# Value stores moved to other queues, two weight loads moved behind the third normalization, and the first tiles normalized in pairs with their root on ScalarE

## The chip, the cores and the metric

The kernel runs on one core of a Trainium2 chip. The metric is the device time of one execution in microseconds (us), and less is better.

The engines are named as in the profile: PE is TensorE (matmuls), PEld its weight loads, DVE is VectorE, ACT is ScalarE, POOL is GpSimd ("Pool" in the text), SP is SyncE, whose queue is called the sync queue here. "ACTq" or "SPq" in a line of the profile is that engine's instruction queue.

## The reference, cut to what matters

The input `x` is 2048 rows of 640. It is normalized once, and two branches read the result: a sliding, dilated attention (32 heads of 20, a window of 8 rows at distance 2) and a gated product of three matrices (F = 1536). Their outputs and `x` are summed.

```python
x  = A_x                                    # (1, 2048, 640) bf16
xn = _layernorm(x)                          # (x - mean) / sqrt(var + 1e-5)
# A: q, k, v = xn @ wqkv; logits over 8 earlier rows (0, 2, ..., 14 back); softmax; weighted v; @ wo
# B: (xn @ w_gate) * (xn @ w_up), then @ w_down
return x + A(xn, wqkv, wo) + B(xn, w_gate, w_up, w_down)
```

## The kernel before: the parts that matter

The 2048 rows are four chunks of four tiles of 128 rows. All engines are scheduled by hand: the program keeps a list for TensorE (`main`), one for VectorE (`chain`) and a list of things that happen when a condition holds (`later`), and a small clock model decides the order in which instructions are emitted. What is emitted on one engine stays in order.

The steps of a chunk that this story needs are:

1. VectorE takes statistics of `x`, Pool takes the root, VectorE scales. The first chunk is transposed on TensorE. Chunks 2 to 4 are stored (`xnD`) and transposed by a DMA (`xnT`).
2. TensorE makes q, k and v. The values go to DRAM (`vD`) and come back, eight shifted rows for each row, as `v8` (two buffers).
3. VectorE multiplies q with eight shifted k (`pw`, eight products a chunk); TensorE adds up the heads (`lps`, called head products here); ScalarE takes the exponential `e`. `e` is stored (`eD`) and comes back transposed by a DMA as `eT`.
4. VectorE normalizes `eT`, then for each tile mixes `v8` with `eT` and adds up. The result is stored and comes back transposed (`oT`) for the output product (`psf`, with `wo_perm`, then `wd`).

```python
    def load_down():
        wo_r = A_wo.rearrange("(h t jl) d -> jl h t d", h=H, t=KT, jl=JL)
        for jl in range(JL):
            nc.gpsimd.dma_start(out=wo_perm[jl * H : (jl + 1) * H, :, :], in_=wo_r[jl])   # 0.8 MB in all
        nc.gpsimd.dma_start(out=wd[:], in_=B_w_down.rearrange("(f p) d -> p f d", p=P))   # 1.9 MB
    # ... cut
            def stats():
                # ... cut: bn_stats, bn_aggr of each tile of the group
                rstd = cpool.tile([P, group], F32, name="rstd", bufs=2)
                nc.gpsimd.tensor_scalar(rstd[:], g["mv"][:, :, 1], EPS, None, op0=ALU.add)
                nc.gpsimd.tensor_tensor(
                    rstd[:], rstd[:], mhalf[:].to_broadcast([P, group]), ALU.pow
                )
                g["rstd"] = rstd
    # ... cut
        if group == 1:               # first chunk: stats 0, stats 1, scale 0, stats 2, scale 1, ...
            prev = None
            for t0 in range(CH):
                cur = steps(t0)
                if prev:
                    prev[0]()
                prev = cur
            prev[0]()
    # ... cut: value product, after the second half of a tile
                    if k == 1:
                        nc.scalar.dma_start(
                            out=vD[HALO + tg * P : HALO + (tg + 1) * P, :], in_=v_t[:]
                        )
    # ... cut
        def keep_e():
            rows = eD[c * 2 * P : (c + 1) * 2 * P, :]
            nc.sync.dma_start(out=rows.rearrange("(g p) t -> p g t", p=P), in_=st["e"][:])
            later.append((turn_e, lambda t=min(clock["pe"], clock["dve"]): t + 3.0))

        def turn_e():
            st["eT"] = apool.tile([P, CH, 2 * P], BF, name="eT")
            rows = eD[c * 2 * P : (c + 1) * 2 * P, :]
            nc.sync.dma_start_transpose(out=st["eT"][:], in_=rows.rearrange("r (t p) -> r t p", p=P))
            done["eT", c] = min(clock["pe"], clock["dve"]) + 7.0
    # ... cut: VectorE's order
    norm(0, 1)
    side(load_ffn)
    norm(1, 4)
    side(constants)
    later.append((lambda: (load_x(2), load_down()), when(("turned", 1))))
    weights(0)
    side(lambda: (want_v8(0), want_v8(1)))
    turned_weights(0)
    norm(2, 4)
    attend(0, range(CH))
    side(lambda: load_x(3))
    weights(1)
    # ... cut: further chunks; TensorE's order:
    vproj(0, range(CH)); qk(0); glu(0); qk(1); vproj(1, range(CH)); qk(2); vproj(2, range(CH)); finish(0)
    # ... cut
```

On VectorE the second chunk's `pw` (`weights(1)`) stands behind all four tiles of the first chunk's attention (`attend(0, ...)`). On TensorE the head products of the second chunk come in as soon as `pw` allows, during or just before `finish(0)`.

The softmax here doesn't subtract the row's maximum and nothing guards it: scores larger than these inputs give would overflow.

## Time and profile before

| | before |
|---|---|
| median of the six runs known at the prediction | 275.74 us (275.15 to 277.23) |
| the run that was profiled | 272.23 us, span 270.5 us |
| PE busy | 261.1 us, 97% |
| query product starts | 17.39 us |
| `eT` lands | 57.06 us (issue 53.56 + 3.5) |
| second chunk's `pw` starts | 87.56 us |

The profiled run is 3.5 us faster than the median.

The page of before. In the rows of slices the span is cut in 40, about 6.8 us each; each digit is a busy share in tenths, PEclk the clock that was granted to TensorE. The last two lines are the chain of work that ended last, by engine and by line.

```profile
span 270.5 us, 4126 instructions
PE 261.1 (97%) x1607; PEld 145.0 (54%) x1624; DVE 202.1 (75%) x258; ACT 101.7 (38%) x181; POOL 34.6 (13%) x72
PEclk9899999999999999999999999999999999999999
DMA  6999999990898975454820896986188498310111
PE 81%; DVE 11%; DMA 5%; SPq 1%; issue 1%; ACT 0%; ACTq 0%
PE psu L556 19%; PE psg L556 19%; PE psf L605 19%; PE psqk L351 8%; PE psf L598 8%; PE psv L377 4%; PE lps L433 4%; DMA v_925<-vD 3%; DVE pw L422 2%; DMA x_t<-in_A_x_dram 2%; DVE v_925 L500 1%; DVE v_607 L500 1%; DVE v_609 L500 1%; DVE v_60
```

PE is busy nearly all the time and carries the chain for 81%. DMA is saturated in the slices from about 7 to 61 us, and idle in the next one.

The head in the timeline of before (start, duration, engine, line, operation, tile; in brackets the idle time before it and what ended it):

```profile
8.26 0.89 DVE L239 BATCH_NORM_STATS2 stats<-x_t 128x6 f32<-128x320 bf16 x2 [2.55 <-DMA x_t<-in_A_x_dram]
9.30 0.39 DVE L261 TENSOR_SCALAR xn_t<-x_t,mv,rstd 128x640 bf16<-128x640 bf16 x1
9.76 0.45 PE L272 MATMUL pst<-ident,xn_t 128*128 128x128 bf16 x5 [1.63 <-DVE xn_t L261]
...
17.39 10.96 PE L351 MATMUL psqk<-xnT,wqkv 128*128 128x512 bf16 x49
```

VectorE works in order. Tile 1's scaling (9.30) was ready by about 6.4 us (its root ends there), but stands behind the statistics of tile 2, whose `x` lands at 8.26. PE waits 1.63 us for it.

The weight loads and the way of the exponentials, in the timeline of before:

```profile
24.62 2.33 POOL L157 DMA_DIRECT2D wo_perm<-in_A_wo_dram  x4
26.94 1.07 POOL L158 DMA_DIRECT2D wd<-in_B_w_down_dram  x1
...
48.91 0.38 SPq L462 DMA_DIRECT2D eD<-e  x1
53.56 1.45 SPq L468 DMA_TRANSPOSE eT<-eD  x1
57.89 1.87 DVE L485 TENSOR_REDUCE rs<-eT 128x128 f32<-128x1024 bf16 x1
```

The weights are issued at 24.6 to 28 us. The exponentials go out at 48.91 and come back transposed at 57.06, and at 57.89 VectorE sums them (`rs`) for its normalization.

The waits of before between 80 and 105 us (who waited for whom: total, times, longest):

```profile
ACT v_t L383 <- DMA oT<-oD: 3.5, 1, 3.5
PE psv L377 <- ACT v_t L383: 1.1, 1, 1.1
PE lps L433 <- DVE pw L422: 0.7, 1, 0.7
```

PE idles 1.8 us here: 1.1 for a PSUM copy that ScalarE does late, and 0.7 for VectorE's `pw`. ScalarE is late because it stands 3.5 us in front of a value store in its queue, and the profile puts this to the landing of an `oT` transpose.

### The profile page before, as it was taken

Reading aid. Unit: us, or ns where it says so; the run is one execution under the profiler, and the core shown is the slowest. Engines: PE = TensorE matmul, PEld = TensorE weight load, DVE = VectorE, ACT = ScalarE, POOL = GpSimd, SP = SyncE. Lnnn points to the kernel's source line nnn. Section 1 sums busy time; section 2 is a strip of 40 time slices with the busy share of each in tenths; the row PEclk is TensorE's granted clock in tenths of the full one; section 3 lists DMA queues with packets and bytes.
Section 4 is the critical chain, followed back from the end, with each engine's and each line's share of the span. In section 5 each row is a group of like instructions: output and inputs, shape, how many; then the busy total and the mean of one; then the engine's idle time right before and its main releaser. Section 6 shows DMA issues by size and latency. Waiting matters only on the chain.

```text
span 270.5 us, 4126 instructions
## 1 busy us (share of the span) xinstructions
PE 261.1 (97%) x1607; PEld 145.0 (54%) x1624; DVE 202.1 (75%) x258; ACT 101.7 (38%) x181; POOL 34.6 (13%) x72
## 2 busy tenths in 40 slices
PE   7799999999999799999999999999999999999995
PEld 7454444444646467644444677744446774445773
DVE  3452796659879996599999979999899979921221
ACT  2455555555653310155555520045551005555000
POOL 3548100400000004300000003020000302000100
PEclk9899999999999999999999999999999999999999
DMA  6999999990898975454820896986188498310111
GB/s 181 332 376 395 257 283 256 377 196 4 224 332 250 270 211 139 157 151 155 262 70 2 262 324 137 266 300 54 39 227 243 128 294 239 125 48 2 48 48 48
DMA packets 54706, 52.18 MB, mean 193 GB/s; under 512 B 24754, under 2 KB 52352, under 8 KB 54688
## 3 DMA queue, kind: packets, MB, share of 16 engines
q1 hardware_dynamic: 49344, 37.82, 51.3%
q0 software_dynamic: 3040, 11.49, 13.3%
q10 hardware_dynamic: 2304, 2.62, 2.7%
q8 instruction: 12, 0.20, 0.3%
q14 instruction: 6, 0.05, 0.1%
HBM read 35.39 MB, written 10.90 MB: 171 GB/s over the span
## 4 chain that ended last, share of the span: by engine, by line
PE 81%; DVE 11%; DMA 5%; SPq 1%; issue 1%; ACT 0%; ACTq 0%
PE psu L556 19%; PE psg L556 19%; PE psf L605 19%; PE psqk L351 8%; PE psf L598 8%; PE psv L377 4%; PE lps L433 4%; DMA v_925<-vD 3%; DVE pw L422 2%; DMA x_t<-in_A_x_dram 2%; DVE v_925 L500 1%; DVE v_607 L500 1%; DVE v_609 L500 1%; DVE v_607 L516 1%; DVE v_925 L516 1%
## 5 line engine op out<-in xcount | busy, mean ns | idle before, releaser
L556 PE MATMUL psu<-xnT,wu 128*128 128x512 bf16 x240 | 59.7, 379 | 0.0
L556 PE MATMUL psg<-xnT,wg 128*128 128x512 bf16 x228 | 59.0, 379 | 0.6
L605 PE MATMUL psf<-wd,hT 128*128 128x320 bf16 x384 | 57.4, 299 | 0.0
L561 ACT CAST gs<-psg 128x512 bf16<-128x512 f32 x48 | 28.1, 585 | 70.7 <-PE psg L556 69.7
L422 DVE TENSOR_TENSOR pw<-qT,kT 128x2560 bf16<-128x2560 bf16 x32 | 46.3, 1485 | 6.8 <-ACT kT L357 6.8
L605 PEld LDWEIGHTS <-hT 128*128 128x128 bf16 x384 | 37.5, 98 | 14.7 <-DVE hT L566 0.2
L351 PE MATMUL psqk<-xnT,wqkv 128*128 128x512 bf16 x195 | 43.9, 379 | 0.3
L556 PEld LDWEIGHTS <-wu 128*128 128x128 bf16 x240 | 23.3, 98 | 28.7 <-issue 0.8
L556 PEld LDWEIGHTS <-wg 128*128 128x128 bf16 x240 | 23.3, 98 | 28.2 <-issue 0.8
L561 ACT CAST us<-psu 128x512 bf16<-128x512 f32 x48 | 28.1, 585 | 25.9 <-PE psu L556 25.9
L566 DVE TENSOR_TENSOR hT<-gs,us 128x512 bf16<-128x512 bf16 x48 | 19.8, 418 | 16.6 <-ACT us L561 16.2
L351 PEld LDWEIGHTS <-wqkv 128*128 128x128 bf16 x200 | 19.4, 98 | 23.6 <-issue 0.8
L622 POOL DMA_DIRECT2D out_dram<-osb x13 | 7.2, 557 | 185.0 <-DVE osb L612 185.0
L612 DVE TENSOR_TENSOR osb<-psf,xr 128x320 bf16<-128x320 f32 x32 | 15.3, 486 | 20.5 <-PE psf L605 17.2
L598 PE MATMUL psf<-wo_perm,oT 128*128 128x320 bf16 x160 | 27.0, 299 | 0.0
L377 PE MATMUL psv<-wqkv,xnT 128*128 128x320 bf16 x160 | 24.4, 308 | 1.2 <-ACT v_t L383 1.1
L239 DVE BATCH_NORM_STATS2 stats<-x_t 128x6 f32<-128x320 bf16 x32 | 13.6, 468 | 9.6 <-DMA x_t<-in_A_x_dram 9.6
L377 PEld LDWEIGHTS <-xnT 128*128 128x128 bf16 x160 | 16.0, 101 | 8.2 <-issue 1.3
L598 PEld LDWEIGHTS <-oT 128*128 128x128 bf16 x160 | 15.5, 98 | 7.1 <-issue 0.8
L383 ACT CAST v_t<-psv 128x320 bf16<-128x320 f32 x32 | 13.3, 426 | 11.9 <-PE psv L377 6.5
L357 ACT CAST qT<-psqk 128x512 bf16<-128x512 f32 x20 | 11.7, 585 | 10.1 <-PE psqk L351 10.1
L357 ACT CAST kT<-psqk 128x512 bf16<-128x512 f32 x20 | 11.7, 585 | 9.9 <-PE psqk L351 9.9
(88 smaller groups left out, 181.7 us busy)
## 6 DMA issues: line engine op xcount, KB each, us to landing
x_t<-in_A_x_dram SPq DMA_DIRECT2D x16, 160.0 KB, 4.3
vD<-v_t ACTq DMA_DIRECT2D x16, 160.0 KB, 5.6
xr<-in_A_x_dram POOLq DMA_DIRECT2D x16, 160.0 KB, 3.7
out_dram<-osb POOLq DMA_DIRECT2D x13, 160.0 KB, 3.2
wg<-in_B_w_gate_dram POOLq DMA_DIRECT2D x2, 960.0 KB, 9.6
wu<-in_B_w_up_dram POOLq DMA_DIRECT2D x2, 960.0 KB, 11.7
xnD<-xn SPq DMA_DIRECT2D x3, 640.0 KB, 4.0
wd<-in_B_w_down_dram POOLq DMA_DIRECT2D x1, 1920.0 KB, 12.7
```

What stands on the lines that cost most here:

```text
L239: nc.vector.bn_stats(s[:, hf, :], x_t[:, hf * N2 : (hf + 1) * N2])
L351: nc.tensor.matmul(ps[:], lhsT=wqkv[:, i, r * D + j * P : r * D + (j + 1) * P], rhs=st["xnT"][:, i, :], start=(i == 0), stop=(i == KT - 1),)
L357: nc.scalar.copy(dst[:, j, o : o + CS], ps[:])
L377: nc.tensor.matmul(ps[:, 0:N2], lhsT=st["xnT"][:, i, tcols(ttl)], rhs=wqkv[:, i, 2 * D + n0 : 2 * D + n0 + N2], start=(i == 0), stop=(i == ...
L383: nc.scalar.copy(v_t[:].rearrange("p (j h) -> p j h", j=Dh)[:, :, k * HH : (k + 1) * HH], ps[:, 0:N2].rearrange("p (h j) -> p j h", j=Dh),)
L422: nc.vector.tensor_tensor(pt[:], st["qT"][:], st["kT"][:, :, off : off + CS], ALU.mult)
L556: nc.tensor.matmul(ps[:], lhsT=w[:, i, f * P : (f + 1) * P], rhs=st["xnT"][:, i, :], start=(i == 0), stop=(i == KT - 1),)
L561: nc.scalar.copy(s[:], ps[:])
L566: nc.vector.tensor_tensor(h[:], st["gu", 0, f][:], st["gu", 1, f][:], ALU.mult)
L598: nc.tensor.matmul(ps[:, 0:N2], lhsT=st["oT", ttl][:, i, :], rhs=wo_perm[:, i, n0 : n0 + N2], start=(i == 0), stop=False,)
L605: nc.tensor.matmul(ps[:, 0:N2], lhsT=st["hT", f][:, tcols(ttl)], rhs=wd[:, f, n0 : n0 + N2], start=False, stop=(f == FT - 1),)
L612: nc.vector.tensor_tensor(osb[:, n0 : n0 + N2], ps[:, 0:N2], xr[:, n0 : n0 + N2], ALU.add)
```

## The change

The intent: (1) normalize the first chunk in pairs of tiles, so that tile 1 does not wait for tile 2's load; (2) take the root of the first pair on ScalarE, with VectorE's reciprocal; (3) load the down and output weights (2.7 MB) behind the third normalization, and the second tile's `v8` behind the issue of `eT`, so that `x`, `v8` and the exponentials' round trip come first; (4) take value stores off ScalarE's queue, onto the sync queue in the first chunk and onto Pool's after it.

```diff
+    root = const.tile([P, 1], F32, name="root")
+    nc.scalar.activation(root[:], eps[:], ACT.Sqrt)
 ...
+                if c == 0 and t0 < 2:
+                    nc.scalar.activation(rstd[:], g["mv"][:, :, 1], ACT.Sqrt, bias=eps[:])
+                    return
 ...
+                    if c == 0 and t0 < 2:
+                        nc.vector.reciprocal(g["rstd"][:], g["rstd"][:])
 ...
         if group == 1:
-            prev = None
-            for t0 in range(CH):
-                cur = steps(t0)
-                if prev:
-                    prev[0]()
-                prev = cur
-            prev[0]()
+            for pair in ((0, 1), (2, 3)):
+                for f in [steps(t0)[0] for t0 in pair]:
+                    f()
 ...
-                        nc.scalar.dma_start(
+                        eng = nc.sync if c == 0 else nc.gpsimd
+                        eng.dma_start(
                             out=vD[HALO + tg * P : HALO + (tg + 1) * P, :], in_=v_t[:]
                         )
 ...
-            done["eT", c] = min(clock["pe"], clock["dve"]) + 7.0
+            done["turned e", c] = min(clock["pe"], clock["dve"])
+            done["eT", c] = done["turned e", c] + 7.0
 ...
-    later.append((lambda: (load_x(2), load_down()), when(("turned", 1))))
+    later.append((lambda: load_x(2), when(("turned", 1))))
+    later.append((load_down, when(("xn", 2, CH - 1))))
     weights(0)
-    side(lambda: (want_v8(0), want_v8(1)))
+    side(lambda: want_v8(0))
+    later.append((lambda: want_v8(1), when(("turned e", 0))))
```

(Cut: the memset of `eps` and the clock model's entries for the ScalarE root.)

## The prediction

> **What bounds the kernel now.** TensorE: the page's busy table gives PE 261.1 of 270.5 us (97%), and the chain of waits is PE for 81%. The busy time per stretch shows where PE is idle: about 3.5 us before 18 us, 1.76 us between 85 and 95 us, about 3.3 us after the last matmul (fixed). A gain can come only from the first two.
>
> *Head.* The timeline shows VectorE, in order, holding tile 1's scaling behind the statistics of tile 2, whose load lands at 8.26 us: the scaling starts at 9.30 although its statistics ended at 5.24. PE does almost nothing from 8.12 to 9.76, then runs at a granted clock of 0.50 to 0.54 from 11 to 14 (the windows). The query product starts at 17.39. [...]
>
> *85 to 95 us.* ScalarE waits 3.5 us in the value store's place in its queue (put down to the oT transpose), so a PSUM copy is late and PE waits 1.07 us; then PE waits 0.7 to 1 us for VectorE's products (pw). VectorE is late because the exponentials' transpose lands at 57.9. DMA is saturated from 7 to 57 us (share 0.9 to 1.13): one xnT transpose takes 8.77 us to issue, the third chunk's x is awaited 2.23 us, and the mask waits behind those statistics.
>
> **What the change does.**
> 1. Tile pairs: stats 0, 1, scale 0, 1. Tile 1's scaling moves from 9.30 to about 6 us. Four value groups (2.7 us) can run between 7.5 and 10.5, while x 2 and 3 arrive. Tile 3's scaling moves only from 11.83 to about 11.4. So the value stage ends near 15 instead of 17.4: 2.3 us gained (1.5 to 3), all on PE's path, partly because the clock falls for less long.
> 2. ScalarE root (estimate 0.25 us) plus reciprocal (0.1 us) for Pool's 0.23+0.58 us: tile 0 is bound by VectorE's statistics of tile 1, so about zero; some 0.3 us for tile 1. Cost: a second table load, 1.28 us in the trace, before the first exponential; the Trainium skill, "ScalarE: Activation LUTs", "What ACT_TABLE_LOAD costs", says about 2.66 us with its drain. ScalarE is 55% busy there and PE has five PSUM buffers: no PE stall.
> 3. Down and output weights (2.7 MB, issued at 24.6 to 28 us) move to about 47 us, towards the free DMA of 60 to 70 us (share 0.2). The transpose, x load, mask and eT come 4 to 7 us earlier; VectorE's attention and second chunk's pw with them.
> 4. Value stores off ScalarE's queue: the 3.5 us block goes; on Pool 0.6 to 1 us each, with slack. The xr loads move behind them, with little harm.
> 3 and 4 together remove about 1.7 us of PE waits (85 to 95 us).
>
> **Sum.** 2.3 + 1.7 = 4.0 us: 275.74 to about **271.7 us**; 8 in 10: 270.2 to 273.6. Chances: faster by over 2% (below 270.2) 0.10, within 2% 0.87, slower 0.03.
>
> **What would show it.** Second scaling near 6 us; query product starting near 15; fewer half-clock slices; two table loads; weight issues near 47; eT landing near 50; no ScalarE wait at 85 to 89; PE idle in 80 to 95 below 0.4 us.
>
> **What would make it wrong.** Clock still half in the value stage (1 us less gain); weights, the second v8 load and transposes colliding at 47 to 60 us and pushing VectorE back; Pool stores stuck behind waits, so v8 loads and residuals late; the whole head idle vanishing (4 us, the upper bound), which alone could reach 2%.

## The result

| | before | after |
|---|---|---|
| median (range, runs) | 275.95 us (272.27 to 279.42, 40) | 277.42 us (275.98 to 278.87, 20) |
| ratio after/before | | 1.0088, 95% interval 1.0067 to 1.0110 |
| the run that was profiled | 272.23 us | 277.93 us |

Ratios are the mean time of one kernel's fast runs over that of the other's of the same rounds, so not quite the ratio of the medians that I quote. A run counts as slow, and enters no ratio, when it is over 1.5% above the fastest of the same kernel. The runs of before spread over more than that (272.27 to 279.42), so one rare fast run of before can push usual ones out of the base. By the ratio the change made the kernel 0.9% slower, by the medians, which leave no run out, 0.5%; both are under the 2% from which a difference is classed as slower. The prediction had 271.7 us and a range up to 273.6, so it was wrong in sign and outside its range, though inside the class "within 2%" that it gave 0.87.

The page of after, the same lines:

```profile
span 276.0 us, 4134 instructions
PE 263.3 (95%) x1607; PEld 145.7 (53%) x1624; DVE 202.6 (73%) x260; ACT 104.0 (38%) x185; POOL 39.1 (14%) x81
PEclk9999999999999779999999999999999999999999
DMA  6999583997697943741950698499169498410111
PE 65%; DVE 17%; DMA 12%; issue 2%; SPq 1%; POOL 0%; ACT 0%; DVEq 0%; ACTq 0%
PE psu L566 16%; PE psg L566 16%; PE psf L615 14%; PE psqk L359 8%; PE psf L608 6%; DMA eT<-eD 4%; PE lps L442 4%; DVE pw L431 4%; DMA v_929<-vD 3%; DMA xr<-in_A_x_dram 2%; PE psv L385 2%; DMA vD<-v_t 2%; DMA x_t<-in_A_x_dram 1%; DVE v_929 
```

The share of PE in the chain fell from 81% to 65%. DVE and DMA took it up, and a single transfer, `eT<-eD`, holds 4% of the span. PEclk is no longer reduced in the second slice, but it is in two slices from about 90 to 104 us.

The head of after, in its timeline:

```profile
5.87 0.45 DVE L273 TENSOR_SCALAR xn_t<-x_t,mv,rstd 128x640 bf16<-128x640 bf16 x1
...
14.97 10.95 PE L359 MATMUL psqk<-xnT,wqkv 128*128 128x512 bf16 x49
```

The head does what the prediction said: the second scaling at 5.87 (said: near 6), the query product at 14.97 (said: near 15), and no half clock.

The loads and the way of the exponentials in after:

```profile
44.17 0.39 SPq L471 DMA_DIRECT2D eD<-e  x1
45.26 2.51 POOL L161 DMA_DIRECT2D wo_perm<-in_A_wo_dram  x4
47.76 1.07 POOL L162 DMA_DIRECT2D wd<-in_B_w_down_dram  x1
...
48.49 2.39 SPq L477 DMA_TRANSPOSE eT<-eD  x1
60.88 1.88 DVE L495 TENSOR_REDUCE rs<-eT 128x128 f32<-128x1024 bf16 x1 [5.33 <-DMA eT<-eD]
```

The weights moved as said (said: near 47), and `eD` and `eT` are issued 4.7 and 5.1 us earlier. But `eT`, said to land near 50, lands at 60.9: VectorE starts its sum `rs` 3 us later than before, after a wait of 5.33 us. The time from issue to landing of `eT`, in the view of that tile, in before:

```profile
DMA to landing us min/median/max: 3.5/3.5/3.5
```

And in after:

```profile
DMA to landing us min/median/max: 12.4/12.4/12.4
```

It is one transfer of 256 KB, and it took 12.4 us instead of 3.5. The `wd` load that was issued just before it took 12.5 us.

The waits of after between 80 and 105 us:

```profile
PE lps L442 <- DVE pw L431: 5.4, 4, 2.6
```

ScalarE's wait of 3.5 us is gone, as said. In its place PE waits 5.4 us, in four pieces, for VectorE's `pw`. The timeline of before there:

```profile
87.56 11.30 DVE L422 TENSOR_TENSOR pw<-qT,kT 128x2560 bf16<-128x2560 bf16 x8
93.30 1.24 PE L433 MATMUL lps<-pw,Ek 128*32 128x512 bf16 x17 [0.69 <-DVE pw L422]
94.47 0.85 PE L598 MATMUL psf<-wo_perm,oT 128*128 128x320 bf16 x5
95.16 2.34 PE L605 MATMUL psf<-wd,hT 128*128 128x320 bf16 x16
```

The timeline of after, the same tiles:

```profile
89.66 11.30 DVE L431 TENSOR_TENSOR pw<-qT,kT 128x2560 bf16<-128x2560 bf16 x8
91.20 0.38 PE L442 MATMUL lps<-pw,Ek 128*32 128x512 bf16 x1 [2.56 <-DVE pw L431]
...
95.40 2.29 PE L442 MATMUL lps<-pw,Ek 128*32 128x512 bf16 x17 [0.82 <-DVE pw L431]
97.63 1.51 PE L608 MATMUL psf<-wo_perm,oT 128*128 128x320 bf16 x5
98.93 3.19 PE L615 MATMUL psf<-wd,hT 128*128 128x320 bf16 x16
```

In both, the last 17 head products start 5.74 us after the first `pw` (93.30 - 87.56 and 95.40 - 89.66): VectorE decides when they run. In after PE arrives earlier, because the head worked, finds nothing to do, and waits. Then it pays again: the same three groups of matmuls take 2.29, 1.51 and 3.19 us where they took 1.24, 0.85 and 2.34, together 2.6 us more. The busy times by stretch show why. The columns are the stretch, its length, busy us of PE, PEld, DVE, ACT and POOL with instruction counts, the granted clock, the DMA share and GB/s.

```profile
92.00:94.00 2.00, 0.38 (x1) 0.09 (x1) 2.00 (x3) 0.00 (x0) 0.00 (x0) 0.96 1.02 378
94.00:96.00 2.00, 1.18 (x9) 0.41 (x12) 2.00 (x2) 0.00 (x0) 0.00 (x0) 0.50 1.07 371
```

PE did almost nothing from 88.6 to 95.4 us, and the clock granted to it was 0.50 when the work came, and still while it ran:

```profile
98.00:100.00 2.00, 2.00 (x10) 1.07 (x8) 2.00 (x3) 0.33 (x1) 0.00 (x0) 0.50 0.94 273
```

The Trainium skill, "TensorE: Matmul & The Clock Gate", "The HAM clock gate", says that the throttled state is the default and that activity releases it. The trace agrees: 0.50 after the wait, full again after 101 us.

### The profile page after: what moved, and what is told of

It reads as the page before. It is cut to its first block, busy times and chain, and to the rows that moved or that the text cites. A ratio compares the mean times of both kernels' runs of the same rounds, so it can differ in the third digit from the quotient of the medians.

```text
span 276.0 us, 4134 instructions
## 1 busy us (share of the span) xinstructions
PE 263.3 (95%) x1607; PEld 145.7 (53%) x1624; DVE 202.6 (73%) x260; ACT 104.0 (38%) x185; POOL 39.1 (14%) x81
## 4 chain that ended last, share of the span: by engine, by line
PE 65%; DVE 17%; DMA 12%; issue 2%; SPq 1%; POOL 0%; ACT 0%; DVEq 0%; ACTq 0%
PE psu L566 16%; PE psg L566 16%; PE psf L615 14%; PE psqk L359 8%; PE psf L608 6%; DMA eT<-eD 4%; PE lps L442 4%; DVE pw L431 4%; DMA v_929<-vD 3%; DMA xr<-in_A_x_dram 2%; PE psv L385 2%; DMA vD<-v_t 2%; DMA x_t<-in_A_x_dram 1%; DVE v_929 L510 1%; DVE v_606 L510 1%
## 5 line engine op out<-in xcount | busy, mean ns | idle before, releaser
L566 PE MATMUL psu<-xnT,wu 128*128 128x512 bf16 x240 | 59.7, 379 | 0.0
L615 PE MATMUL psf<-wd,hT 128*128 128x320 bf16 x384 | 58.3, 302 | 0.0
L608 PE MATMUL psf<-wo_perm,oT 128*128 128x320 bf16 x160 | 27.6, 304 | 0.0
L385 PE MATMUL psv<-wqkv,xnT 128*128 128x320 bf16 x160 | 22.7, 299 | 0.0
L442 PE MATMUL lps<-pw,Ek 128*32 128x512 bf16 x160 | 12.8, 408 | 5.7 <-DVE pw L431 5.7
L397 POOL DMA_DIRECT2D vD<-v_t x12 | 6.5, 544 | 77.5 <-ACT v_t L391 77.5
## 6 DMA issues: line engine op xcount, KB each, us to landing
wu<-in_B_w_up_dram POOLq DMA_DIRECT2D x2, 960.0 KB, 12.5
wd<-in_B_w_down_dram POOLq DMA_DIRECT2D x1, 1920.0 KB, 12.5
```

Of the source, the lines that this page charges most:

```text
L385: nc.tensor.matmul(ps[:, 0:N2], lhsT=st["xnT"][:, i, tcols(ttl)], rhs=wqkv[:, i, 2 * D + n0 : 2 * D + n0 + N2], start=(i == 0), stop=(i == ...
L442: nc.tensor.matmul(lps[H * j : H * (j + 1), :], lhsT=Ek[:, i, :], rhs=st["pw", g, j][:, i, :], start=(i == 0), stop=(i == KT - 1), tile_po ...
L566: nc.tensor.matmul(ps[:], lhsT=w[:, i, f * P : (f + 1) * P], rhs=st["xnT"][:, i, :], start=(i == 0), stop=(i == KT - 1),)
L608: nc.tensor.matmul(ps[:, 0:N2], lhsT=st["oT", ttl][:, i, :], rhs=wo_perm[:, i, n0 : n0 + N2], start=(i == 0), stop=False,)
L615: nc.tensor.matmul(ps[:, 0:N2], lhsT=st["hT", f][:, tcols(ttl)], rhs=wd[:, f, n0 : n0 + N2], start=False, stop=(f == FT - 1),)
```

## The experiments

Eighteen kernels ran; one is the kernel before. Each profile gave the start of the query product, the issue and landing of `eT`, and the start of the second chunk's `pw`. Ratios are against before in the same rounds.

| kernel | query | `eT` issued | landed (took) | `pw` 2nd chunk | profiled us / span | median us | ratio [95%] |
|---|---|---|---|---|---|---|---|
| before | 17.39 | 53.56 | 57.06 (3.5) | 87.56 | 272.23 / 270.5 | 275.95 | |
| b1_before_again | 17.39 | 56.40 | 61.10 (4.7) | 91.63 | 276.56 / 274.6 | one run | |
| after | 14.97 | 48.49 | 60.89 (12.4) | 89.66 | 277.93 / 276.0 | 277.42 | 1.0088 [1.0067, 1.0110] |
| e1_down_old | 14.92 | 51.70 | 55.80 (4.1) | 86.36 | 272.10 / 270.1 | 272.31 | 0.9915 [0.9841, 0.9990] |
| e2_down_only | 15.86 | 49.39 | 62.39 (13.0) | 91.71 | 277.02 / 275.0 | 277.46 | 1.0140 [1.0071, 1.0208] |
| e3_down_gated | 14.74 | 48.27 | 52.67 (4.4) | 88.65 | 275.89 / 274.2 | 276.32 | 1.0006 [0.9960, 1.0051] |
| e4_head_only | 15.04 | 57.06 | 61.26 (4.2) | 91.21 | 276.19 / 274.1 | 276.42 | 1.0092 [1.0026, 1.0158] |
| e5_pairs_only | 15.20 | 56.27 | 59.97 (3.7) | 89.68 | 275.23 / 273.2 | 275.86 | 0.9989 [0.9949, 1.0029] |
| e6_stores_only | 17.10 | 53.54 | 56.94 (3.4) | 87.65 | 273.08 / 271.3 | 277.74 | none |
| e7_v8_early | 14.71 | 48.24 | 60.44 (12.2) | 90.40 | 278.29 / 276.4 | 278.06 | 1.0063 [1.0023, 1.0103] |
| e8_gate33 (slow) | 14.62 | 52.34 | 57.14 (4.8) | 89.51 | 279.55 / 277.8 | 276.48 | 1.0057 [0.9998, 1.0116] |
| e9_gate36 | 15.03 | 53.89 | 57.19 (3.3) | 88.41 | 275.54 / 273.8 | 275.53 | 1.0035 [0.9992, 1.0078] |
| e10_eT_first | 15.14 | 46.53 | 54.13 (7.6) | 86.03 | 273.17 / 271.2 | 275.30 | 1.0008 [0.9960, 1.0055] |
| e11_wd_early | 14.62 | 48.15 | 54.05 (5.9) | 84.89 | 269.95 / 268.2 | 270.46 | 0.9854 [0.9808, 0.9900] |
| e12_wd_early_eT_first | 14.69 | 46.06 | 54.66 (8.6) | 85.17 | 270.41 / 268.5 | 271.03 | 0.9866 [0.9820, 0.9912] |
| e13_pool_root | 14.46 | 47.98 | 54.38 (6.4) | 85.00 | 271.85 / 269.8 | 270.42 | 0.9846 [0.9802, 0.9890] |
| e14_act_stores | 14.80 | 48.33 | 54.63 (6.3) | 85.90 | 270.88 / 268.8 | 271.36 | 0.9879 [0.9835, 0.9923] |
| e15_no_pairs | 15.63 | 49.15 | 54.75 (5.6) | 85.86 | 271.69 / 269.7 | 271.51 | 0.9894 [0.9849, 0.9938] |
| e16_loads_only | 16.11 | 49.63 | 56.53 (6.9) | 86.05 | 271.03 / 269.0 | 271.20 | 0.9865 [0.9837, 0.9893] |
| e17_wd_early_v8_early (slow) | 14.61 | 50.41 | 56.21 (5.8) | 87.77 | 274.55 / 272.6 | 271.74 | 0.9847 [0.9803, 0.9891] |

Two profiles fell into the slow state (e8 and e17). In the 18 others, and in e17's, the span minus the start of that `pw` lies between 182.9 and 186.3 us (before: 270.5 - 87.56 = 182.9; after: 276.0 - 89.66 = 186.3; e11: 268.2 - 84.89 = 183.3). Where the query starts hardly enters: e4 starts it 2.35 us before the kernel before and has the same 182.9.

One caution on the ratios of e1, e2 and e4: in their rounds the fastest run of before took 271.90 us, so six of its eleven runs (276.25 and up) count as slow and left the base. By the medians of all runs (before 276.25) e1 is at 0.986, e2 at 1.004 and e4 at 1.001.

### First four: which part costs the time?

**Theory A**: the weights on Pool's queue slow `eT`. **Theory B**: the second `v8` load, now later, is the harm. **Theory C**: the head itself harms, by the ScalarE root or by running ahead into transfers (e6's expectation uses C for harm by the stores on Pool). **Theory D**: VectorE's chain, not TensorE, decides when the second chunk's head products run, so the head's lead turns into a wait.

**e1_down_old**: after, with the weights back at their old place.

```diff
-    later.append((lambda: load_x(2), when(("turned", 1))))
-    later.append((load_down, when(("xn", 2, CH - 1))))
+    later.append((lambda: (load_x(2), load_down()), when(("turned", 1))))
```

> The change, but the down and output weights loaded where before.py loads them (with the third chunk's x). Theory A (the moved weights share the DMA engines with the first exponentials' transpose, eT, which then takes 12.4 us instead of 3.5, and everything of VectorE up to the second chunk's pw is late): eT takes under 6 us from issue to landing, TensorE waits under 1 us for pw at the second chunk's head products, ratio to before about 0.985. Rival B (eT is late because of the new order of the sync queue: value stores, second v8 load behind it): eT still takes 10 us or more, ratio about 1.005. Rival D (VectorE's chain, not TensorE, decides when the second chunk's head products run, so the head's 2.4 us turn into a wait there, also with a quick eT): eT lands at 56 to 58 as before, TensorE waits 2 to 4 us for pw, ratio 0.995 to 1.0.

Measured: 272.31 us, ratio 0.9915; `eT` takes 4.1 us and lands at 55.80, and `pw` starts at 86.36. PE still waits 2.4 us for `pw` (A said under 1, D said 2 to 4). Two of its six runs were slower (277.62 and 275.24), and the interval is wide. Undoing this one part takes away the loss and leaves a small gain over before.

**e2_down_only**: before, with only the weights moved (the reverse edit of e1).

```diff
-    later.append((lambda: (load_x(2), load_down()), when(("turned", 1))))
+    later.append((lambda: load_x(2), when(("turned", 1))))
+    later.append((load_down, when(("xn", 2, CH - 1))))
```

> The kernel before, with nothing but the load of the down and output weights moved behind the third normalization. Theory A: eT takes 8 us or more, lands near 59 to 61, TensorE waits 2 us or more for pw, ratio 1.01 to 1.02. Rival B: eT under 6 us and landing near 50, ratio 0.995 to 1.0.

Measured: 277.46 us, ratio 1.014, but 0.4% by the medians (see the caution above). The transfer is as A said:

```profile
DMA to landing us min/median/max: 13.0/13.0/13.0
```

PE waits 5.8 us, not for `pw` as expected, but for ScalarE's copy behind the value store, as in b1 below. The move alone makes the slow `eT`. e1 and e2 are the two halves of one test, and both go with A; how much of the time the move alone costs, e2 leaves between 0.4 and 1.4%.

**e4_head_only**: before, with pairs and the ScalarE root, and nothing else of the change. As an edit of after, three of its hunks are undone:

```diff
-    later.append((lambda: load_x(2), when(("turned", 1))))
-    later.append((load_down, when(("xn", 2, CH - 1))))
+    later.append((lambda: (load_x(2), load_down()), when(("turned", 1))))
 ...
-    side(lambda: want_v8(0))
-    later.append((lambda: want_v8(1), when(("turned e", 0))))
+    side(lambda: (want_v8(0), want_v8(1)))
 ...
-                        eng = nc.sync if c == 0 else nc.gpsimd
-                        eng.dma_start(
+                        nc.scalar.dma_start(
```

> The kernel before with the head alone (tile pairs, first root on ScalarE); weights, v8 loads and value stores as before. The glu starts 2.4 us earlier in every theory (25.5 instead of 28.0). If the head's gain stays (theory A): ratio 0.990 to 0.992. If it turns into a wait for pw at the second chunk's head products (rival D): TensorE waits there 2.5 to 3.5 us, ratio 0.997 to 1.0.

Measured: 276.42 us, ratio 1.0092. The query starts at 15.04, yet nothing is gained; by the medians nothing is lost either (276.42 against 276.25). As D said, the lead turns into a wait, though not one for `pw`: ScalarE waits 7.9 us in front of the third chunk's first value store and PE 5.5 us for it; `pw` starts only at 91.21.

**e6_stores_only**: before, with only the value stores moved.

```diff
-                        nc.scalar.dma_start(
+                        eng = nc.sync if c == 0 else nc.gpsimd
+                        eng.dma_start(
```

> The kernel before with the value stores alone moved (sync queue for the first chunk, Pool for the rest). ScalarE's 3.5 us block and TensorE's 1.07 us wait behind it at 89 us go. If VectorE's chain decides (rival D) the wait for pw grows by the same 1 us: ratio 0.998 to 1.002. If not: ratio about 0.996. If Pool stores harm by themselves (rival C, late v8 loads or residuals): 1.005 or more.

Measured: the profiled run took 273.08 us, and the other five 277.21 to 278.37. They count as slow beside the first, so there is no ratio. The profile shows ScalarE's wait gone and 1.9 us of PE waiting for `pw` instead. For the time this run is inconclusive.

### Next four: is it the weights, and what did the head do?

**e3_down_gated**: after, with the weights held until `eT` has been normalized, by one-column writes of VectorE into both tiles.

```diff
+        def gate():
+            nc.vector.memset(wo_perm[:, 0, 0:1], 0.0)
+            nc.vector.memset(wd[:, 0, 0:1], 0.0)
+            load_down()
 ...
+        if c == 0:
+            op(chain, ("gate", c), gate, 0.1)
```

(Cut: the line that loads the weights behind the third normalization is taken out.)

> The change, but the down and output weights also wait for two one-column writes of VectorE that stand behind the normalization of eT, so that they start only when eT has landed (near 55 us). Theory A: eT takes under 6 us and lands near 51 to 53 (60.9 in the change), the second chunk's pw is done before TensorE asks for it, TensorE idles under 0.5 us from 80 to 95 us, span near 266, ratio to before 0.975 to 0.985. Rival B (sync queue order): eT late as in the change, ratio about 1.005. Rival A2 (the weights' 2.7 MB hurt wherever they stand in this stage, now through the second v8 load or the xnT transpose): eT early, but VectorE waits over 2 us for a v8 tile, ratio 0.99 to 1.0.

Measured: 276.32 us, ratio 1.0006: a miss for the time. `eT` is well (4.4 us, landed 52.67), but the weights, now issued at 59.7 to 63 us, meet the next transfer. In the timeline of e3:

```profile
62.09 1.07 POOL L162 DMA_DIRECT2D wd<-in_B_w_down_dram  x1
65.61 0.39 SPq L411 DMA_DIRECT2D v<-vD  x1
77.11 2.83 DVE L517 TENSOR_TENSOR v<-v,eT 128x5120 bf16<-128x5120 bf16 x1 [6.33 <-DMA v<-vD]
```

The third `v8` load, issued at 65.61, is awaited until 77.11, and VectorE loses 6.33 us there. The stretch that looked free in the profile of before (no traffic from 61 to 68 us) ended where VectorE's next `v8` load was issued, at 68.26; in e3 the chain is ahead and issues it inside. This is the same harm as in A, to another small transfer that the same chain waits for.

**e5_pairs_only**: before, with pairs alone and the root on Pool.

```diff
-            prev = None
-            for t0 in range(CH):
-                cur = steps(t0)
-                if prev:
-                    prev[0]()
-                prev = cur
-            prev[0]()
+            for pair in ((0, 1), (2, 3)):
+                for f in [steps(t0)[0] for t0 in pair]:
+                    f()
```

> The kernel before with the tile pairs alone, first root on Pool as before. If the pairing makes the head's gain and the ScalarE root next to nothing: glu starts 25.6 to 26.2 (25.55 in the change, 27.97 before), one table load. If the root on ScalarE is needed: 26.5 or later. Time as with the head alone (1.009), because TensorE waits at the value store's block near 85 to 92 us: 1.000 to 1.010.

Measured: 275.86 us, ratio 0.9989. The query starts at 15.20, and nothing comes of it: ScalarE waits 6.8 us before the value store, PE 4.4 us.

**e7_v8_early**: after, with the second `v8` load back at its old place.

```diff
-    side(lambda: want_v8(0))
-    later.append((lambda: want_v8(1), when(("turned e", 0))))
+    side(lambda: (want_v8(0), want_v8(1)))
```

> The change with the second v8 load put back where before.py has it (ahead of eT on the sync queue). Rival B (its new place delays eT or VectorE): ratio 0.99 or less. Theory A (weights): eT still 9 us or more, ratio within 0.5% of the change's, 1.004 to 1.012.

Measured: 278.06 us, ratio 1.0063; `eT` takes 12.2 us. B falls.

**b1_before_again**: before, unchanged.

> The kernel before, unchanged, for a second profile: its profile on record is of a run of 272.2 us, when its median is near 276. If the usual run is one where eT lands later and ScalarE's value store therefore waits longer for the oT transpose: run of 275 to 277 us, ScalarE's block at 85 to 92 us 6 to 8 us long (3.5 on record), TensorE waits 4 to 6 us for it (1.07 on record). If the run is a fast one again, this stays open.

Measured: 276.56 us in the profiled run. Its timeline:

```profile
91.63 5.69 DVE L422 TENSOR_TENSOR pw<-qT,kT 128x2560 bf16<-128x2560 bf16 x4
91.90 0.33 ACTq L388 DMA_DIRECT2D vD<-v_t  x1
92.32 0.76 ACT L383 CAST v_t<-psv 128x320 bf16<-128x320 f32 x2 [6.64 <-DMA oT<-oD]
92.80 1.37 PE L377 MATMUL psv<-wqkv,xnT 128*128 128x320 bf16 x5 [4.19 <-ACT v_t L383]
```

This is the same program as before, with the same head, and yet `eT` lands at 61.1 instead of 57.1 and PE waits 4.19 us instead of 1.07. Here `eD` is issued at 48.71, as before, but takes 7.6 us to land, while `eT` needs 4.7 us. The profile that the prediction read was of a rare, fast run: of the 40 timed runs of before, two are under 273 (272.27 and 272.37). It shows the idle time of PE between 80 and 105 us as 1.8 us where the more usual run has 4.2.

Against this more usual run, after did not lose time at `eT`: it lands at 61 in both, although after issues it 8 us earlier. What the slow transfer did was to take that lead away. PE then comes to the same wait with the head's lead and spends it: in the 20 us from 84 on, b1 has 4.2 us of idle PE and after 5.4. After ends its first head products at 97.7 and b1 at 98.6, so 0.9 us of the lead is left; and then the half clock of after, which falls later, stretches the next two groups by 1.5 us (0.66 + 0.85, above), where b1 does the same two at full clock (its own slow stretch came before). At the next head products after is 0.55 us behind b1 (104.36 against 103.81), and at the last of the fourth chunk 1.2 us (196.38 against 195.18); the spans differ by 1.4. In between, the trace of after has one more wait of PE for `pw`, 0.27 us at 189.71, which b1 does not have; the rest was not followed up.

This run also corrected a reading. The profile puts ScalarE's wait to an `oT` transpose. But that transpose lands after the store has been issued: in before at 84.14 + 5.1 = 89.24 us, the store at 88.78. What landed just before the store is the `v8` load of the second chunk's first tile: in before at 82.14 + 6.6 = 88.74 us. In b1 it is 85.62 + 6.2 = 91.82 and the store 91.90, in e4 85.46 + 6.2 = 91.66 and 91.74, and the four other profiles with the stores on ScalarE's queue (e2, e5, e14, e16) agree: in all seven the store is issued 0.04 to 0.12 us after that landing, and before the landing of `oT`. That load is issued when VectorE is done with the third tile, so this wait too ends when VectorE's chain allows. The link may be a completion semaphore that the two DMAs share; I read that in the instructions of the built program, and no run took the semaphore away. So the link is not shown; the agreeing times are.

### Third four: where should the weights go?

**e8_gate33** and **e9_gate36**: after, with the weights held behind an earlier step of VectorE (the fourth and the sixth `pw` of the first chunk), and `eT` put ahead of the third chunk's store.

```diff
+                if (c, g, j) == (0, 0, 3):      # e9: (0, 1, 1)
+                    op(chain, ("gate", c), gate, 0.1)
 ...
-                            later.append((keep, lambda t=t: t))
+                            first = [("turned e", 0)] if c == 2 else []
+                            later.append((keep, lambda t=t: max(t, when(*first)())))
```

> The change, with the down and output weights started between the two groups of pw of the first chunk (near 33 us, by the same one-column writes of VectorE) and eT's transpose put ahead of the third chunk's xn store on the sync queue. The stretch from 36 to 46 us has free DMA in the change (share 0.23 in 40 to 45 us). Theory A: weights land by 44 us, eT lands near 50 to 52, no v8 load over 8 us, pw of the second chunk begins by 84 us (89.7 in the change), TensorE idles under 0.5 us from 80 to 100 us, span near 266, ratio to before 0.965 to 0.980. If the head and the value stores were worth nothing by themselves: ratio 0.99 or more although eT is early.

Measured: 276.48 us, ratio 1.0057. In its (slow) profile the weights were issued at 33.5 to 37 us and the `eD` store, at 44.33, took 8 us to land beside `wd`, which landed at 50.0; so `eT` was issued only at 52.34. The expectation took 36 to 46 us of after as free, but the DMA share there was 0.85 from 36 to 40.

> As the run before, with the weights started three products of pw later (near 36 us). Theory A: the same within 0.5% if the weights land before eT's transpose is issued (46 us); if they still run then, eT takes 2 to 5 us longer and the ratio is 0.5 to 1.5% higher.

Measured: 275.53 us, ratio 1.0035. The weights were issued from 37.0 us (the edit moves them two products of `pw`, not three), `wd` landed at 53.6, and `eD` took 9.6 us. Both are misses: the weights again met a small transfer that the chain needs, this time `eD`.

**e10_eT_first**: after, with only the second hunk of that edit, so that `eT` goes ahead of the third chunk's store.

```diff
-                            later.append((keep, lambda t=t: t))
+                            first = [("turned e", 0)] if c == 2 else []
+                            later.append((keep, lambda t=t: max(t, when(*first)())))
```

> The change with eT's transpose put ahead of the third chunk's xn store on the sync queue, weights where the change has them (45 us). eT is issued near 46.5 instead of 48.5. If the place on the sync queue matters (2 us earlier) and the weights do not: eT lands by 52, ratio 0.99 or less. Theory A: the weights' transfers hold eT all the same; it lands at 56 or later, ratio 0.998 to 1.008.

Measured: `eT` is issued 2 us earlier than in after, takes 7.6 us beside the weights, and `pw` starts at 86.03; the profiled run took 273.17 us, but the five others 275.06 to 276.02, ratio 1.0008. Better than after, and still no gain over before.

**e11_wd_early**: after, with `wd` (1.9 MB) loaded at the old place and only `wo_perm` (0.8 MB) late.

```diff
+    def load_wd():
         nc.gpsimd.dma_start(out=wd[:], in_=B_w_down.rearrange("(f p) d -> p f d", p=P))
 ...
-    later.append((lambda: load_x(2), when(("turned", 1))))
+    later.append((lambda: (load_x(2), load_wd()), when(("turned", 1))))
     later.append((load_down, when(("xn", 2, CH - 1))))
```

> The change with the down weights (1.9 MB) loaded where before.py has them and the output weights (0.8 MB) alone behind the third normalization. Theory A, by dose: eT's time falls from 12.4 us to about 4 to 6 us, as the output weights have landed (4 us each) before or just after it is issued; ratio 0.985 to 0.995. If any part of the move is enough to hold eT: still 9 us or more, ratio 1.00 or more.

Measured: 270.46 us (269.95 to 272.35), ratio 0.9854: the best version, faster than both kernels. The waits of e11 between 80 and 105 us:

```profile
PE lps L444 <- DVE pw L433: 1.6, 2, 1.0
```

The busy times of e11 from 84 to 104 us, with the columns as above:

```profile
84.00:104.00 20.00, 18.36 (x153) 11.71 (x152) 18.77 (x29) 3.17 (x7) 6.08 (x11) 1.00 0.79 225
```

The same stretch of before:

```profile
84.00:104.00 20.00, 18.24 (x153) 11.72 (x152) 19.76 (x28) 4.79 (x11) 0.77 (x2) 1.00 0.81 243
```

The same stretch of after:

```profile
84.00:104.00 20.00, 14.57 (x92) 8.28 (x89) 19.15 (x19) 2.72 (x6) 3.33 (x7) 0.83 0.79 246
```

With 0.8 MB beside it, `eT` takes 5.9 us, and because it is issued 5.4 us earlier than in before it still lands 3 us earlier. PE is busy 18.36 of the 20 us at full clock; in after it is 14.57 at 0.83. The head is still in place here, so C falls too.

### Last six: which parts of the change earn anything, once `eT` is early?

Each takes one part out of e11, or puts e11's loads alone into before.

**e12_wd_early_eT_first**: e11 with `eT` ahead of the third chunk's store (the hunk of e10).

```diff
-                            later.append((keep, lambda t=t: t))
+                            first = [("turned e", 0)] if c == 2 else []
+                            later.append((keep, lambda t=t: max(t, when(*first)())))
```

> The version with the down weights early (0.985 to before), with eT's transpose ahead of the third chunk's xn store. If the sync queue's order and the output weights still hold eT: eT lands 2 us earlier (near 53 instead of 55.1), the 1.6 us of TensorE idle at 85 to 95 us shrinks to 0.5, ratio 0.979 to 0.984. If not: 0.985 to 0.990.

Measured: 271.03 us, ratio 0.9866. `eT` is issued 2.1 us earlier than in e11, but takes 8.6 us and lands no sooner. A miss.

**e13_pool_root**: e11 with the first pair's root back on Pool.

```diff
-    nc.scalar.activation(root[:], eps[:], ACT.Sqrt)
 ...
-                if c == 0 and t0 < 2:     # at all three places
+                if False:
```

> The version with the down weights early, first root on Pool again (pairs kept, one table load). As predicted (the root is worth 0.0 to 0.3 us): ratio 0.985 to 0.988. If the root on ScalarE costs by its second table load: 0.982 or less. If it is worth over 1 us: 0.990 or more.

Measured: 270.42 us, ratio 0.9846, the same as e11. The ScalarE root is worth nothing that can be measured.

**e14_act_stores**: e11 with the value stores back on ScalarE's queue.

```diff
-                        eng = nc.sync if c == 0 else nc.gpsimd
-                        eng.dma_start(
+                        nc.scalar.dma_start(
```

> The version with the down weights early, value stores on ScalarE's queue again. As predicted the store in ScalarE's queue blocks until an oT transpose has landed: ScalarE blocked 4 to 7 us near 85 us, TensorE waiting 2 to 5 us for it, ratio 0.995 to 1.003. If the stores' place does not matter: 0.984 to 0.989.

Measured: 271.36 us, ratio 0.9879. ScalarE's wait is back with 4.0 us and costs PE 1.6 us, but the waits for `pw` shrink to 1.0. The loss against e11, 0.25% by the ratios, is within their intervals.

**e15_no_pairs**: e11 with the old order of the first chunk's tiles.

```diff
-            for pair in ((0, 1), (2, 3)):
-                for f in [steps(t0)[0] for t0 in pair]:
-                    f()
+            prev = None
+            for t0 in range(CH):
+                cur = steps(t0)
+                if prev:
+                    prev[0]()
+                prev = cur
+            prev[0]()
```

> The version with the down weights early, tiles normalized one after the other as in before.py. The query product starts 2.3 us later (17.2 instead of 14.9). If the head's gain comes through to the end: ratio 0.992 to 0.995. If VectorE's chain hides most of it: 0.985 to 0.990, with less TensorE idle at 85 to 95 us.

Measured: 271.51 us, ratio 0.9894. The query starts at 15.63, not near 17 as I expected: without the slowed clock that before has from 12 to 14 us, the old order reaches it only 1.0 us later than e11. Not resolved from e11 by the intervals.

**e16_loads_only**: before, with e11's load placement (`wd` early, `wo_perm` and the second `v8` load late) and no head, root or store change.

```diff
+    def load_wd():
         nc.gpsimd.dma_start(out=wd[:], in_=B_w_down.rearrange("(f p) d -> p f d", p=P))
 ...
-            done["eT", c] = min(clock["pe"], clock["dve"]) + 7.0
+            done["turned e", c] = min(clock["pe"], clock["dve"])
+            done["eT", c] = done["turned e", c] + 7.0
 ...
-    later.append((lambda: (load_x(2), load_down()), when(("turned", 1))))
+    later.append((lambda: (load_x(2), load_wd()), when(("turned", 1))))
+    later.append((load_down, when(("xn", 2, CH - 1))))
 ...
-    side(lambda: (want_v8(0), want_v8(1)))
+    side(lambda: want_v8(0))
+    later.append((lambda: want_v8(1), when(("turned e", 0))))
```

> The kernel before with the second v8 load behind eT and the output weights alone behind the third normalization; head, root, value stores and down weights as before. If the rest of the gain is in these two: eT lands by 56 (57.9 and about 60.5 in the two profiles of before), ratio 0.988 to 0.994. If the parts only help together: 0.997 to 1.003.

Measured: 271.20 us (270.69 to 272.25), ratio 0.9865. The placement of the loads alone makes nearly the whole gain of e11.

**e17_wd_early_v8_early**: e11 with the second `v8` load at its old place.

```diff
-    side(lambda: want_v8(0))
-    later.append((lambda: want_v8(1), when(("turned e", 0))))
+    side(lambda: (want_v8(0), want_v8(1)))
```

> The version with the down weights early, second v8 load back ahead of eT on the sync queue. If its place matters: eT's store and transpose take longer behind 1.3 MB more on the same queue, eT lands 2 to 4 us later (57 to 59), TensorE idles 3 us or more at 85 to 95 us, ratio 0.992 to 1.000. If not: 0.985 to 0.988.

Measured: 271.74 us, ratio 0.9847. Its median holds slower runs (up to 277.23) that the ratio leaves out. By the ratio, the later second `v8` load does nothing; it may make the slower runs rarer, which six runs cannot show.

## Why the prediction was wrong, point by point

- **What bounds the kernel.** The page says PE, 97% busy, and that is true for most of the span. But the prediction priced a gain at the head as if PE alone decided when everything later runs. Around 90 us PE waits for VectorE's chain: `eT` lands, VectorE normalizes, mixes four tiles, and only then makes the second chunk's `pw`. From the start of `rs` to that `pw` it takes 29.7 us in before (57.89 to 87.56), 28.8 in after (60.88 to 89.66), and about 30 in e11. This chain does not care when the query started.
- **Item 1, the head: right where it was measured, wrong in the sum.** The query product came at 14.97 (said: near 15), 2.4 us earlier. Of these 2.4 us nothing reached the end by itself: e5, with the head alone, is at 0.9989, and e16, without any of it, has 0.9865 beside e11's 0.9854. "All on PE's path" was the error: PE only arrives earlier at the same wait. Besides, kernels with the old order start the query at 15.6 to 16.1 us when the clock does not fall (e2, e15, e16), so pairs are worth 1.0 to 2.4 us even there. In e2 and e16 PE waits the same 1.63 us for tile 1 as in before, and the clock stays at 1.00 from 11 to 15 us where before has 0.50 to 0.75; so this wait alone does not bring the half clock, and part of the 2.4 us is luck.
- **Item 2, the root: about right.** Predicted about zero; e13 against e11 shows none. The second table load is there (1.28 us at 35.26 us in after), and the exponential starts 0.01 us after it.
- **Item 3, the weights: the step that failed.** The prediction said that they "move to about 47 us, towards the free DMA of 60 to 70 us" and that `eT` would land near 50. They were issued at 45.3 to 48.8, `wd` 0.7 us in front of `eT` at 48.49, which then took 12.4 us for what had taken 3.5, and landed at 60.9. That is 3.8 us later than in the profiled run of before and no earlier than in b1, so the 4 to 7 us that everything on VectorE was to gain did not come. The free stretch existed, but the load, which itself takes 12.5 us, had to cross the one transfer on which VectorE waited to get there. e2 shows the slow `eT` from this part alone, e1 shows it gone without it, and the time 5 us shorter than after's. The prediction did name this collision among the things that would make it wrong, and gave it no weight in the range.
- **Item 4, the value stores: the wait went, the gain did not come.** ScalarE's 3.5 us are gone as said. PE then waits for `pw`, which was next in line and is on the same VectorE chain; "PE idle below 0.4 us" became 5.4. And the half clock that follows that wait costs 2.6 us against the profiled run of before (b1 runs slowed for a while too: 0.91 over 84 to 104 us, after 0.83).
- **The base.** The idle time that the prediction set out to remove was read from a run of 272.23 us, against a median of 275.74. A more usual run (b1) has 4.2 us of idle there, not 1.8. A sum that starts from the one and is taken from the other does not hold.
- **The size of the gain.** 4.0 us was there to be had: e11 is 4.0 us under the base of the prediction by its ratio (0.0146 x 275.2 us, the median of before in that batch). But it goes with an earlier `eT` and `pw` (54.05 and 84.89), not with the sum that I wrote down; that the sizes agree is chance.

What stays open:

- Whether e4 is worse than e5 at all. The ratios say so (1.0092 and 0.9989), but e4's base had lost six of eleven runs and e5's none; by the medians they are at 1.001 and 0.998. e4's profile has a 0.7 us PE wait behind a ScalarE that waits 4.8 us for VectorE, and e13 shows no effect of the root in e11.
- What tips the runs of before between about 272 and 275 to 278 us. In the two profiles the landing of `eD` and `eT` differs by 4 us; what decides that is not shown.
- How much the head earns in e11. Its loss without pairs, 0.4% by the ratios, lies within the intervals.
- e11 still has 1.6 us of waits for `pw`; no version removed them.
- Why e10 gains nothing, though its profile has `eT` at 54.13 and `pw` at 86.03, nearly as e11. That profile is of its fastest run by 1.9 us; none shows the others.
- How e16's gain divides. It moves `wo_perm` and the second `v8` load; no run moves `wo_perm` alone in before. By e17's ratio the `v8` load adds nothing in e11.

## What to carry to other kernels

Before you price a gain on the busiest engine, find the next wait of that engine and ask which chain ends it: a gain in front of such a wait is spent waiting, unless the chain moves too. Before you move a large load into a stretch that looks free, list the small transfers that a chain waits for in and before that stretch, after the change has shifted them: here 2.7 MB hit `eT`, then `v8`, then `eD`, at each later place where they were put whole, and splitting them (1.9 MB early, 0.8 MB late) was what worked. Compare the profiled run's time with the median before you read idle times from it, and look how many runs of the base a ratio leaves out.

## What the Trainium skill lacked or had wrong

- "DMA: Bandwidth & Descriptors", "Issuing engines are not separate DMA queues", says that DMAs of the scalar, sync and gpsimd engines run on the same 16 DMA engines and interleave. The runs agree: the first `eT` on the sync queue took 12.2 to 13.0 us where it was issued just after `wd` on Pool's queue (after, e2, e7), 7.6 us where it was issued 1.4 us before `wd` (e10), and 3.3 to 4.8 where these weights were not loaded just then (before, b1, e1, e3 to e6, e8, e9). The section gives no size of the harm; here, a 256 KB transpose took as long as the 1.9 MB load beside it (12.5 us in after), and 5.6 to 8.6 us when only the 0.8 MB were beside it (e11 to e16).
- "Advanced Engine Details and Errata", "X-Bar Transpose (TRN2)", says "TRN2 transpose DMAs are as fast as regular DMAs". Here the fourth chunk's transpose `eT` took 3.2 to 3.5 us in all twenty profiles, and the plain store of the same 256 KB to `eD` just before it 2.1 to 2.2 us. One reads DRAM and the other writes it, and some other traffic runs beside the transpose, so this is no clean comparison.
- "ScalarE: Activation LUTs", "What ACT_TABLE_LOAD costs", gives 1283 ns for the load, and the trace shows 1.28 us. Its drain, with which a switch comes to about 2.7 us, is not to be seen here: the load starts at 35.26 us, 0.02 us after the ScalarE instruction before it has ended, and the exponential at 36.55, 0.01 us after the load's end.
- No page says that the issue of a DMA can wait for the landing of another queue's transfer that it has nothing to do with. Here a value store on ScalarE's queue was issued at 88.78 us, when a `v8` load of the sync queue had landed at 88.74, and likewise in six more profiles; that a shared completion semaphore ties them is my reading of the built program and not shown by a run.
